# One store per output tile over both 64-row parts, and a last tile that two engines copy out

## The chip, the cores and the metric

The kernel runs on one core of a Trainium2 chip. The metric is the device time of one execution in microseconds (us), the median of several runs. Three runs of the kernel before took 406.9, 407.35 and 407.36 us. One execution was also taken with the hardware profiler; its span is 407.7 us at a mean granted TensorE clock of 0.99, and all times of single instructions come from it.

## The reference

Attention without softmax over 8 batches of 12 heads (448 tokens, head size 64), then a gated feed-forward layer. In short:

```
scores = q @ k.T / 8                       # per batch and head
attn   = maximum(scores, 0)**2 / 448
x      = (attn @ v), heads side by side    # 3584 tokens x 768
gate   = maximum(x @ w_gate, 0)            # 768 x 1536
val    = x @ w_val                         # 768 x 1536
out    = (gate * val) @ w_out              # 1536 x 768, result 3584 x 768 in float32
```

## The kernel before

**Stages.** All engines' programs are written out by the kernel's own planner (`plan`, from L174): it is given operations with their engine, an estimated time, what they depend on, and which buffers they take and read, and it commits one after the other. The instructions are then emitted in order of the planned start. Each engine runs its own list in that order, and waits at an instruction until what it depends on is done. An operation that takes a buffer (`alloc`) waits for the last reader of what was in it.

The batches go in pairs through attention (scores L681, relu L692 or L694, square L704 or L706, product with v L723), the two input products of the feed-forward layer (L787 and L896) and the output product (L1013). From batch 2 on, q and k are transposed by DMA, issued from SyncE (L612). The pairs overlap in time: while the output product of one pair runs, attention of a later one does too.

**Output.** A tile of the result has 128 rows by 384 columns (half of the 768). Its 128 partitions are two groups of 64 tokens. The rows of a batch are laid out so that token `p*7 + t` of the batch is partition p of slot t (`rows`, L973), so a group's 64 rows stand 7 rows apart in the result, and the two groups of a tile are two slots: of the same batch, next to each other, or in some tiles of two batches. There are 56 tiles. The output product of a block of two such tiles is made by a scheme with seven products in place of eight (`out_both`, from L1020), with sums and differences of the hidden tiles (`sh`, L1098, on VectorE), and it ends in one of two ways:

- `evac_add` (L1000): VectorE adds a saved part to what stands in PSUM, and writes a tile `o` in SBUF (L1003).
- `evac` (L992): VectorE or ScalarE, as the planner chooses, copies PSUM to `o` with a scale (`copy_out`, L840; L845 is ScalarE's form, L849 VectorE's).

There are five `o` buffers (the sixth number of `BUFFERS`, L79).

**Stores.** Both ways call `store` (L976), which issues two transfers for a tile, one per group of 64 rows. For most tiles both come from SyncE. For the last four tiles (`last`, L980) the first comes from SyncE and the second from ScalarE. The planner reckons 0.6 us of the issuing engine for each transfer, and 2.5 us until it lands. The last tile of all is written by `evac`, called in `p3_of` (L1125).

Of the kernel before, what the change touches and what calls it, by code (L numbers as in the profile page):

```python
# [57 lines left out]
class Planner:  # L58
# [20 lines left out]
    BUFFERS = (3, 11, 3, 5, 4, 5, 3)  # L79
    PV_PAIRS = (0, 0)  # L80
    JOIN = True
    TWO_QUEUES = True
    SCORES_FIRST = 0.0
    SPLIT = False
    MERGE = False
# [241 lines left out]
def kernel(  # L327
# [10 lines left out]
    nc = tc.nc  # L338
# [3 lines left out]
    B, H, S, D = q.shape  # L342
# [5 lines left out]
    NT = S // P2  # L348
# [7 lines left out]
    OH = d_model // 2  # L356
# [7 lines left out]
    out_scale = lam * lam  # L364
# [7 lines left out]
    ps = psum.tile([128, 8, 512], FP32, name="ps")  # L372
# [19 lines left out]
    o_t = [pool.tile([128, OH], FP32, name=f"o{i}") for i in range(N_O)]  # L392
# [3 lines left out]
    r_x, r_f, r_g, r_o = Res(N_X), Res(N_F), Res(N_G), Res(N_O)  # L396
# [21 lines left out]
    others, pool_ops = [], []  # L418
# [421 lines left out]
    def copy_out(eng, dst, src, scale=None):  # L840
        if eng == "ACT":
            if scale is None:
                nc.scalar.copy(dst, src)  # L843
            else:
                nc.scalar.activation(out=dst, in_=src, func=AF.Copy, scale=float(scale))  # L845
        elif scale is None:
            nc.vector.tensor_copy(dst, src)
        else:
            nc.vector.tensor_scalar_mul(dst, src, float(scale))  # L849
# [123 lines left out]
    def rows(b):  # L973
        return out[b * S:(b + 1) * S, :].rearrange("(p t) m -> t p m", t=NT)

    def store(ob, op, where):  # L976


        slots, hf = where
        last = slots[1] in (((B - 3, 0), (B - 1, 0)) if Planner.JOIN else ((B - 1, NT - 1), (B - 2, NT - 2))) if Planner.TWO_QUEUES else slots[1] == (B - 1, NT - 1)  # L980

        def emit(queue, zs):
            for z in zs:
                bb, t = slots[z]
                queue.dma_start(out=rows(bb)[t][:, hf * OH:(hf + 1) * OH], in_=o_t[ob.idx][64 * z:64 * z + 64])

        for eng, queue, zs in (("SP", nc.sync, (0,)), ("ACT", nc.scalar, (1,))) if last else (("SP", nc.sync, (0, 1)),):
            st = Op({eng: (0.6 * len(zs),) * 2}, lambda queue=queue, zs=zs: emit(queue, zs), deps=[op], reads=[ob])
            st.land = 2.5
            others.append(st)  # L990

    def evac(pb, dep, where, engs=None):  # L992
        ob = Buf(r_o)
        op = Op({"ACT": A384, "DVE": V384}, None, deps=[dep], alloc=[ob], reads=[pb])
        op.emit = lambda: copy_out(op.eng, o_t[ob.idx], ps[:, pb.idx, :OH], out_scale)
        others.append(op)
        store(ob, op, where)
        return op

    def evac_add(pb, dep, fop, fb, where):  # L1000

        ob = Buf(r_o)
        op = Op({"DVE": V384}, lambda: nc.vector.scalar_tensor_tensor(  # L1003
            o_t[ob.idx], ps[:, pb.idx, :OH], float(out_scale), f_t[fb.idx][:, :OH], ALU.mult, ALU.add),
            deps=[dep, fop], alloc=[ob], reads=[pb, fb])
        others.append(op)
        store(ob, op, where)
        return op

    def out_mm(lhs, rhs, pb, start, deps, seg, alloc=(), reads=(), grp=None):  # L1010
        def emit():
            for kf in range(FH):
                nc.tensor.matmul(ps[:, pb.idx, :OH], lhsT=lhs(kf), rhs=rhs(kf), start=start and kf == 0,  # L1013
                                 stop=kf == FH - 1, skip_group_check=True)

        return pe(emit, mm_time(FH, OH), deps=deps, alloc=list(alloc), reads=list(reads), grp=grp)
# [3 lines left out]
    def out_both(b, seg, T_ops):  # L1020
# [11 lines left out]
        nblk = NC + joined  # L1032
# [13 lines left out]
        def tail():  # L1046
            lhs = lambda par: lambda kf: hT[:, 2 * kf + par, S - P2:S + P2]
            A, Bk = bank(), bank()
            slots = ((b, NT - 1), (b + 1, 0))
            even, odd = h_of(pr, (0, 0), (1, 0)), h_of(pr, (0, 1), (1, 1))  # L1050
            a0 = out_mm(lhs(0), w(0, 0), A, True, even + wd, seg, [A], [hb], grp=(pr, "t"))
            fop, fb = snapshot(A, a0, OH, out_scale)
            b0 = out_mm(lhs(0), w(0, 1), Bk, True, even + wd + T_ops, seg, [Bk], [hb], grp=(pr, "t"))

            def rest():
                a1 = out_mm(lhs(1), w(1, 0), A, False, odd + [fop], seg, [], [hb], grp=(pr, "t"))
                b1 = out_mm(lhs(1), w(1, 1), Bk, False, odd + [b0], seg, [], [hb], grp=(pr, "t"))
                evac(A, a1, (slots, 0))
                evac_add(Bk, b1, fop, fb, (slots, 1))
                made.update({(0, "c"): a1, (0, "d"): b1})  # L1060

            made.update({(0, "a"): a0, (0, "b"): b0})
            return rest
# [13 lines left out]
        prev = None  # L1077
        for i in range(nblk + 1):
            cur = None
            if i < nblk:  # L1080
# [11 lines left out]
                for n, a, c, f, parts in (  # L1092
# [4 lines left out]
                    dep = {1: [0], 2: [1]}.get(n, [])  # L1097
                    op = Op({"DVE": (0.46, 0.58)}, lambda n=n, a=a, c=c, f=f: nc.vector.tensor_tensor(sh[n], a(), c(), f),  # L1098
                            deps=of(*parts) + [S_ops[d] for d in dep] + ([prev["S"][n]] if prev and joined else []), alloc=[shb[n]],
                            reads=[hb] + [shb[d] for d in dep])  # L1100
# [6 lines left out]
                           s=tokens,  # L1107
# [14 lines left out]
            def p3_of(prev, i=i):  # L1122
                p3 = made[(i - 1, "3")] = out_mm(prev["sx"](2), w(1, 1), prev["A"], False, [prev["S"][2], o22], seg, [], [prev["shb"][2]],
                            prev["gr"](3))
                evac(prev["A"], p3, (prev["s"][0], 1))  # L1125

            if cur is not None:
                p7 = made[(i, "7")] = out_mm(sx_(3), tw(1), cur["D"], True, T_ops + [S_ops[3]], seg, [cur["D"]], [shb[3]], gr(7))
                cur["p7op"], cur["p7b"] = snapshot(cur["D"], p7, OH, out_scale)
                p2 = made[(i, "2")] = out_mm(hx(1, 0), w(1, 0), cur["E"], True, of((0, 1)) + wd, seg, [cur["E"]], [hb], gr(2))  # L1130
                evac_add(cur["E"], p2, sop, sb, (cur["s"][0], 0))
                if prev is not None:
                    p3_of(prev)
                p6 = made[(i, "6")] = out_mm(sx_(1), tw(0), cur["A"], False, T_ops + [S_ops[1], sop], seg, [], [shb[1]], gr(6))
                cur["uop"], ub = snapshot(cur["A"], p6, OH, out_scale)
                p4 = made[(i, "4")] = out_mm(hx(1, 1), tw(2), cur["D"], False, of((1, 1)) + T_ops + [cur["p7op"]], seg, [], [hb], gr(4))
                evac_add(cur["D"], p4, cur["uop"], ub, (cur["s"][1], 0))
            else:
                p3_of(prev)
            in_order(i)  # L1140
            prev = cur
# [149 lines left out]
```

## Time and profile before

| engine or part | busy us of 407.7 | what it does |
|---|---|---|
| TensorE | 397.1 | all products |
| VectorE | 324.9 | relu, squares, sums, copies |
| ScalarE | 263.0 | relu, squares, copies |
| GpSimd | 75.6 | issues the loads |
| DMA queue 1 (SyncE), all 16 engines | 28.3% | transposes and stores |
| DMA queue 10 (ScalarE), all 16 engines | 0.3% | four stores |
| DMA queue 0 (GpSimd), all 16 engines | 44.0% | loads |

The busy time of an engine is the sum of its instructions' times; a share of DMA is the time that packets took, over the span of 16 DMA engines. These are means over stages with different work. The stores fall in four stretches, about 113 to 150 us, 213 to 251, 309 to 330 and 380 to 405. A VectorE write of an `o` tile takes 557 ns (41 of them), a ScalarE one 490 ns (15). The last store is issued at 404.12 us.

### The profile page before, as it was taken

The page shows a single profiled execution, that of the slowest core. Times are in us where ns is not written, and L with a number is a line of the kernel's source. Part 1 is how long each engine was busy: PE and PEld are TensorE (multiplying, and loading weights), DVE is VectorE, ACT ScalarE, POOL GpSimd, SP SyncE. Part 2 cuts the span into 40 slices and gives each one's busy share as a digit, 9 for nine tenths or more (in the row PEclk, how much of TensorE's full clock was granted, in tenths as well). Part 3 has the DMA queues.
Part 4 walks back from the last instruction along what each step waited for, and adds up shares of the span by engine and source line. Part 5 has one row for each costly group of instructions (what it writes and reads, how often), then busy time and mean ns, then how long its engine had stood idle before and what let it go on. Part 6 is the DMA issues. An engine that isn't in the chain of part 4 may idle for free.

```text
span 407.7 us, 8763 instructions
## 1 busy us (share of the span) xinstructions
PE 397.1 (97%) x3460; PEld 207.2 (51%) x3460; DVE 324.9 (80%) x570; ACT 263.0 (65%) x395; POOL 75.6 (19%) x121
## 2 busy tenths in 40 slices
PE   8789999999999999999999999999999999999995
PEld 4587744444445544444454544444445555555663
DVE  4988674998688798999897998898799657677652
ACT  3878873896686886878587887476686544343221
POOL 7856142122211222102122112110000000000000
PEclk9969999999999999999999999999999999999999
DMA  9999999998779997688878999542002430000244
GB/s 116 187 197 199 200 131 169 159 150 102 92 110 183 142 182 99 74 99 113 82 102 143 168 176 170 76 50 36 2 1 55 100 80 0 2 0 2 72 113 127
DMA packets 77305, 43.44 MB, mean 107 GB/s; under 512 B 40912, under 2 KB 77264, under 8 KB 77264
## 3 DMA queue, kind: packets, MB, share of 16 engines
q0 software_dynamic: 34896, 23.60, 44.0%
q1 hardware_dynamic: 42048, 18.89, 28.3%
q8 instruction: 27, 0.44, 0.4%
q10 hardware_dynamic: 320, 0.39, 0.3%
q14 instruction: 14, 0.11, 0.1%
HBM read 47.19 MB, written 11.01 MB: 143 GB/s over the span
## 4 chain that ended last, share of the span: by engine, by line
PE 91%; DMA 3%; DVE 3%; ACT 2%; issue 0%; ACTq 0%; SPq 0%; DVEq 0%
PE ps L896 36%; PE ps L1013 24%; PE ps L787 12%; PE ps L681 9%; PE ps L723 8%; DMA qkT<-perm 3%; PE ps L1169 2%; ACT at L692 2%; DVE at L694 1%; PE ps L535 1%; PE ps L582 1%; DVE at L706 1%; DVE xT L740 0%; DVE o L1003 0%; DVE hT L938 0%
## 5 line engine op out<-in xcount | busy, mean ns | idle before, releaser
L692 ACT ACTIVATE at<-ps 128x896 bf16<-128x896 f32 (+4 forms) x109 | 94.8, 907 | 17.1 <-PE ps L681 17.0
L843 ACT COPY f<-ps 128x448 f32<-128x448 f32 x100 | 52.8, 531 | 55.3 <-PE ps L896 52.0
L694 DVE TENSOR_SCALAR at<-ps 128x896 bf16<-128x896 f32 (+4 forms) x62 | 66.4, 1073 | 9.5 <-PE ps L681 6.5
L704 ACT ACTIVATE at<-at 128x896 bf16<-128x896 bf16 (+3 forms) x71 | 65.3, 937 | 2.1 <-DVE at L694 1.6
L706 DVE TENSOR_TENSOR at<-at 128x896 bf16<-128x896 bf16 (+3 forms) x100 | 59.0, 613 | 1.1 <-ACT at L692 0.9
L681 PE MATMUL ps<-qkT 64*64 64x448 bf16 (+2 forms) x756 | 51.8, 349 | 3.0 <-DMA qkT<-perm 1.0
L896 PE MATMUL ps<-xT,gvT 128*128 128x448 bf16 x216 | 52.8, 353 | 0.0
L896 PE MATMUL ps<-sx,wv 128*128 128x448 bf16 x216 | 52.2, 353 | 0.0
L896 PE MATMUL ps<-xT,wg 128*128 128x448 bf16 x216 | 51.7, 353 | 0.2 <-DVE at L694 0.2
L896 PEld LDWEIGHTS <-gvT 128*128 128x128 bf16 x324 | 30.0, 98 | 32.6 <-issue 6.9
L1013 PEld LDWEIGHTS <-sh 128*128 128x128 bf16 x312 | 29.2, 98 | 23.7 <-issue 4.2
L422 POOL DMA_DIRECT2D raw<-in_k_dram x18 | 11.3, 628 | 138.9 <-DVE perm L606 113.5
L723 PE MATMUL ps<-at,vv 64*64 64x448 bf16 (+2 forms) x700 | 34.7, 335 | 1.2 <-ACT at L704 0.8
L422 POOL DMA_DIRECT2D vv<-in_v_dram x44 | 26.6, 616 | 49.0 <-PE ps L681 46.4
L1013 PEld LDWEIGHTS <-hT 128*128 128x128 bf16 x270 | 25.5, 98 | 19.9 <-issue 3.6
L1013 PE MATMUL ps<-wo,hT 128*128 128x384 bf16 x192 | 35.5, 327 | 0.0
L681 PEld LDWEIGHTS <-qkT 64*64 64x64 bf16 x756 | 18.9, 109 | 29.3 <-issue 24.5
L845 ACT ACTIVATE f<-ps 128x384 f32<-128x384 f32 x37 | 18.1, 490 | 23.9 <-PE ps L1013 21.0
L787 PE MATMUL ps<-xT,wg 128*128 128x448 bf16 (+2 forms) x180 | 32.7, 319 | 0.3 <-DVE at L694 0.3
L938 DVE TENSOR_TENSOR hT<-ps,g 128x448 bf16<-128x448 f32 x36 | 22.4, 622 | 13.1 <-PE ps L896 12.9
L787 PE MATMUL ps<-xT,wv 128*128 128x448 bf16 (+2 forms) x180 | 32.2, 315 | 0.0
L1003 DVE SCALAR_TENSOR_TENSOR o<-ps,f 128x384 f32<-128x384 f32 x41 | 22.7, 554 | 11.0 <-PE ps L1013 10.2
(70 smaller groups left out, 496.8 us busy)
## 6 DMA issues: line engine op xcount, KB each, us to landing
out_dram<-o SPq DMA_DIRECT2D x108, 96.0 KB, 2.2
vv<-in_v_dram POOLq DMA_DIRECT2D x44, 112.0 KB, 6.9
raw<-in_k_dram POOLq DMA_DIRECT2D x18, 224.0 KB, 4.8
raw<-in_q_dram POOLq DMA_DIRECT2D x18, 224.0 KB, 7.0
wo<-in_moe_w_out_dram POOLq DMA_DIRECT2D x4, 576.0 KB, 12.0
wg<-in_moe_w_gate_dram POOLq DMA_DIRECT2D x5, 384.0 KB, 9.3
wv<-in_moe_w_val_dram POOLq DMA_DIRECT2D x5, 384.0 KB, 10.4
gvT<-in_k_dram POOLq DMA_DIRECT2D x6, 224.0 KB, 6.9
```

What stands on the lines that cost most here:

```text
L422: op = Op({"POOL": (0.5 + 0.0004 * n_desc,) * 2}, lambda: nc.gpsimd.dma_start(out=dst(), in_=src), deps=deps, alloc=alloc)
L681: nc.tensor.matmul(banks()[64 * j:64 * j + 64, z, h2], lhsT=self.k_of(j, h2, k), rhs=self.q_of(j, h2), start=True, stop=True)
L692: nc.scalar.activation(self.at_of(i, m), banks(), AF.Relu)
L694: nc.vector.tensor_scalar_max(self.at_of(i, m), banks(), 0.0)
L704: nc.scalar.activation(a, a, AF.Square)
L706: nc.vector.tensor_tensor(a, a, a, ALU.mult)
L723: nc.tensor.matmul(ps[64 * h2:64 * h2 + 64, ps2.idx + j, :n], lhsT=st.v_of(j, h2, c), rhs=self.at_of(c)[64 * j:64 * j + 64, 0, h2], start= ...
L787: nc.tensor.matmul(ps[:, pb.idx, z * n:(z + 1) * n], lhsT=w[:, kd, fc], rhs=xT_t[xbuf[b].idx][:, kd, cols], start=(kd == 0), stop=(kd == K ...
L843: nc.scalar.copy(dst, src)
L896: nc.tensor.matmul(ps[:, pb.idx, :S], lhsT=w(g)[:, fc], rhs=rhs, start=start and g == 0, stop=stop and g == KH - 1, skip_group_check=True)
L1003: op = Op({"DVE": V384}, lambda: nc.vector.scalar_tensor_tensor(o_t[ob.idx], ps[:, pb.idx, :OH], float(out_scale), f_t[fb.idx][:, :OH], AL ...
L1013: nc.tensor.matmul(ps[:, pb.idx, :OH], lhsT=lhs(kf), rhs=rhs(kf), start=start and kf == 0, stop=kf == FH - 1, skip_group_check=True)
```

## The change

Each tile is stored by one transfer, whose destination is given as an access pattern of two groups by 64 rows by the columns, and whose source is the whole tile of 128 partitions. It takes the place of two issues per tile, and of the special case for the last four tiles. The last tile is copied out by two engines at the same time: VectorE takes the left 192 columns and SyncE stores them, ScalarE takes the right 192 and stores them itself. This is meant to shorten the end of the program, and to halve the issuing work of the queues. The two halves take an `o` buffer each.

```diff
-    TWO_QUEUES = True
...
-    def store(ob, op, where):
+    def store(ob, op, where, eng="SP", cols=(0, OH)):
         slots, hf = where
-        last = slots[1] in (((B - 3, 0), (B - 1, 0)) if Planner.JOIN else ((B - 1, NT - 1), (B - 2, NT - 2))) if Planner.TWO_QUEUES else slots[1] == (B - 1, NT - 1)
-
-        def emit(queue, zs):
-            for z in zs:
-                bb, t = slots[z]
-                queue.dma_start(out=rows(bb)[t][:, hf * OH:(hf + 1) * OH], in_=o_t[ob.idx][64 * z:64 * z + 64])
-
-        for eng, queue, zs in (("SP", nc.sync, (0,)), ("ACT", nc.scalar, (1,))) if last else (("SP", nc.sync, (0, 1)),):
-            st = Op({eng: (0.6 * len(zs),) * 2}, lambda queue=queue, zs=zs: emit(queue, zs), deps=[op], reads=[ob])
-            st.land = 2.5
-            others.append(st)
+        c0, c1 = cols
+
+        def emit():
+            lo, hi = (rows(bb)[t][:, hf * OH + c0:hf * OH + c1] for bb, t in slots)
+            dst = bass.AP(lo.tensor, lo.offset, [[hi.offset - lo.offset, 2]] + [list(x) for x in lo.ap])
+            (nc.scalar if eng == "ACT" else nc.sync).dma_start(out=dst, in_=o_t[ob.idx][:, c0:c1])
+
+        st = Op({eng: (0.6, 0.6)}, emit, deps=[op], reads=[ob])
+        st.land = 2.5
+        others.append(st)
...
-    def evac(pb, dep, where, engs=None):
+    def evac(pb, dep, where, last=False):
+        for eng, queue, c, t in (("DVE", "SP", 0, (0.27, 0.36)), ("ACT", "ACT", OH // 2, (0.24, 0.36))) if last else ():
+            cols = (c, c + OH // 2)
+            ob = Buf(r_o)
+            op = Op({eng: t}, lambda eng=eng, cols=slice(*cols), ob=ob: copy_out(
+                eng, o_t[ob.idx][:, cols], ps[:, pb.idx, cols], out_scale), deps=[dep], alloc=[ob], reads=[pb])
+            others.append(op)
+            store(ob, op, where, queue, cols)
+        if last:
+            return
...
-                evac(prev["A"], p3, (prev["s"][0], 1))
+                evac(prev["A"], p3, (prev["s"][0], 1), b == B - 2 and i == nblk)
```

Apart from this, the instructions of TensorE, VectorE, ScalarE and GpSimd stand in the same order in both programs; SyncE's list is the same with one store where there were two.

## The prediction

> **What bounds the kernel now.** I read the busy shares first, then the table of 40 slices, then the stages in which results are stored, and the end of the chain of waits last.
>
> ```profile
> PE 397.1 (97%) x3460; PEld 207.2 (51%) x3460; DVE 324.9 (80%) x570; ACT 263.0 (65%) x395; POOL 75.6 (19%) x121
> PE   8789999999999999999999999999999999999995
> DMA  9999999998779997688878999542002430000244
> out_dram<-o SPq DMA_DIRECT2D x108, 96.0 KB, 2.2
> ```
>
> TensorE is busy 97% and no slice but the first few and the last leaves it idle: it sets the time. The stores are 108 transfers on SyncE and 4 on ScalarE, landing 2.2 us after issue. The DMA row shows where they fall: beside the loads in slices 12 to 15 and 21 to 25, and alone in slices 31 to 33 and 38 to 40. The next view splits the span at these stages (columns: stretch, length, busy time and count of each engine, clock, DMA share, GB/s).
>
> ```profile
> 113.00:150.00 37.00, 36.88 (x321) 17.91 (x317) 32.30 (x63) 28.12 (x42) 7.30 (x12) 1.00 0.95 151
> 213.00:251.00 38.00, 38.00 (x359) 18.78 (x358) 34.26 (x60) 30.05 (x43) 8.52 (x14) 1.00 1.01 160
> 309.00:330.00 21.00, 21.00 (x155) 11.50 (x154) 15.60 (x33) 9.56 (x16) 0.00 (x0) 1.00 0.41 100
> 380.00:405.00 25.00, 23.27 (x144) 13.79 (x141) 12.20 (x23) 6.37 (x13) 0.00 (x0) 1.00 0.48 119
> ```
>
> The four output stages hold 14, 14, 12 and 16 of the 56 tiles (28, 28, 24 and 32 transfers; each tile is two). In the last two the DMA engines are under half busy, so stores cost TensorE nothing: it is busy 21.00 of 21.00 us. Last, the chain in the final 10 us:
>
> ```profile
> 402.31 0.02 issue
> 402.33 0.57 DVE o L1003
> 402.90 0.02 issue
> 402.93 0.50 ACTq L985
> ...
> 403.60 0.49 ACT o L845
> ```
>
> ScalarE issues a store at 402.93, and only then copies the last tile, from 403.60; its store is issued at 404.12, and the span ends at 407.7. Everything after TensorE's end (402.13 + 1.14 = 403.27) is 4.4 us.
>
> **What the Trainium skill says.** (1) "DMA: Bandwidth & Descriptors", section "Why a DMA increments its semaphore by 16 and not by 1": a DMA is cut along the slowest non-size-1 dimension of its source and of its destination, over the largest number of DMA engines, at most 16, that divides both; for SyncE and ScalarE these are the lowest-numbered ones. The trace agrees for 64-row stores: each left 64 packets of 1,536 bytes and sixteen of 4 bytes, one per engine. It has no outer dimension below 16, so it doesn't show the other half of the rule. (2) The same page, "Rules for kernel authors", advises one 128-partition transfer in place of two over halves of the partitions, because both use the same engines. That speaks for the change, if the one transfer also uses all 16. (3) "Specifications" there: about 27 GiB/s per engine. 65 ns for 1,536 bytes, the commonest packet time on the ScalarE queue in the trace, is 23.6 GB/s, a little less.
>
> **The change, part by part.**
>
> *One store per tile.* The source is 128 partitions. The destination is now [2, 64, 384], with the two row groups outermost, because their distance isn't a multiple of the row step. By (1) the engine count is the largest that divides 128 and 2, which is **two**. The same 196,608 bytes then go as 64 packets on each of two engines, where four packets of each of two transfers went to each of 16. Nothing in the trace shows a two-engine transfer, so I bound a packet: 65 ns with little beside it; and from the stages with stores alone, 0.48 x 16 x 25 us = 192 us for 119 GB/s x 25 us / 1,536 B = 1,937 packets, 99 ns with 16 engines at work. The skill's 27 GiB/s gives 53 ns. I take 65 ns, as fourteen engines are now quiet: **4.16 us per tile** on the same two engines, ends 3.4 and 6.3 us. A tile arrives about every 1.6 us in the last two stages (25 us / 16, 21 us / 12), so stores become the bound there.
>
> *What waits.* There are five o buffers. A copy into one waits until the store of five tiles earlier has landed. That copy stands in VectorE's (or ScalarE's) program order ahead of the sums `sh` of the next block and of the relus and squares, and TensorE waits for those. So the wait passes on to all engines almost whole. On SyncE, DMA transposes stand behind the stores, in the queue and on the two engines.
>
> *Last stage.* First store issued at 380.6; first packet 1.1 us after issue (404.12 to 405.24 for the last store). Five buffers keep the two engines fed. 16 x 4.16 = 66.6, so data ends at 448.3; in the trace the last packet (406.1) precedes the end by 1.6 us: 449.9 against 407.7, **+42**.
>
> *Third stage.* Only the wait for buffers counts, since the rest drains behind the next matmuls. The 12th copy (329.3) needs the 7th landing: 309.4 + 1.1 + 7 x 4.16 + 0.2 = 339.8, **+10.5**.
>
> *First and second stage.* The 14th copy (146.8 and 246.3) needs the 9th landing, 9 x 4.16 = 37.4 us of engine time. But the two engines also carry their sixteenth of the loads and transposes. At the shortest usual time of each packet size in the trace, these fill 0.45 and 0.50 of an engine there, 17 and 19 us. First: 113.5 + 1.1 + 37.4 + 17 = 169, **+22**. Second: 213.3 + 1.1 + 37.4 + 19 = 270.8, **+24.5**. With engines otherwise idle these would be +5 and +6. What is left drains in the 63 us between them.
>
> *Fewer issues.* An issue takes SyncE about 0.55 us; 52 fewer transfers save 29 us on an engine that mostly waits. Nothing, hidden by TensorE. A late effect would be earlier transposes, lost behind the above.
>
> *Last tile in two halves, and ScalarE's issues gone.* ScalarE no longer issues three stores ahead of its last copy, so it can start at about 403.3, not 403.6. The halves cost roughly 0.49 - 192 x 0.64 ns = 0.37 us on ScalarE (slope from 531 ns for 448 columns and 490 for 384) and about the same on VectorE; both then store side by side. Before, the issue came at 404.12; now at about 403.7: **-0.4**, but with two engines the last issue isn't on the path, as the queue ahead of it is 20 us deep. So it is worth nothing in the main case.
>
> Sum: 407.35 + 42 + 10.5 + 22 + 24.5 = 506, say **506 us**.
>
> **The rivals.**
>
> *A: 16 engines after all,* if the program loaded on the chip cuts the two groups differently. Then every store lands in about the 2.2 us of now, TensorE's work is unchanged (the order of all engines' other instructions is the same in both programs), and only -0.4 us of the tail remains: 406.9, at most some tenths lower if transposes issued earlier help. For it: it is what the change wants, and no run here contradicts it. Against it: the rule read literally. This is the rival on the other side, not slower.
>
> *B: two engines, but the first two stages hide it,* because loads run well ahead and leave the two engines alone: only the last two stages and +5 and +6 count, 407.35 + 42 + 10.5 + 11 = 471. With the fast end of a packet (3.4 us per tile) the last stage costs 16 x 0.76 = 12 less, the third +5 and the first two nothing: about 442. Against it: a DMA share of 0.95 and 1.01 in these stages.
>
> *C: two engines, and it compounds.* Transposes wait behind up to five stores, and loads finish only when their shares on these two engines do; the scores of a group of heads begin some 11 us after the first of its two transposes is issued (120.9 to 132.2), a few us after the second lands, which is less than one store. If each of the first two stages costs 25 us more, 556. At 99 ns a packet (6.3 us per tile) the last stage alone is +76, the third +26; with the first two at 60 together, 569.
>
> **How the numbers follow.** I give the main case 0.45, B 0.20, C 0.20 and A 0.15: the rule is stated for this queue and shape, but no run here shows it. The range leaves out A and the far end of C: from 442, the fast end of B, to 575, beyond C's sum. Slower has the three cases with two engines, 0.85. A lies at -0.1% of 407.35, mostly within 0.2% (0.81 us): same 0.09, faster 0.06.
>
> **What would show it.** Right: stores landing in 6 us and more where 2.2 stood, 20 when queued; a DMA share of 2/16 = 0.12 through the last stage with GB/s near 47; copies into o waiting for DMA out_dram<-o by tens of us in total; the chain ending in stores, not in TensorE. The packets would keep 1,536 bytes and their number, but completions would be two 4-byte packets per store. If the stretch from 380 is 25 us long again and stores land in some 2.5 us, the engine count was wrong and A holds. If stores take 6 us and more, but the first two stages keep their length, B; if transposes take 20 us and scores wait for them, C.

## The result, and the profile after

| | median, us | runs |
|---|---|---|
| before | 407.55 | 6 |
| changed | 527.28 | 6 |

The ratio is 1.289, with a 95% interval of 1.2825 to 1.2963: 120 us slower. The profiled run of the changed kernel has a span of 521.7 us.

The same lines of its page as were shown of before (busy times; the slices of TensorE and of the DMA engines), with the granted clock added:

```profile
PE 419.1 (80%) x3460; PEld 210.7 (40%) x3460; DVE 326.8 (63%) x571; ACT 262.7 (50%) x395; POOL 75.8 (15%) x121
PE   8799999999567379999937693999995999995500
PEclk9999999999779879999996896999996999996755
DMA  9999999779866685677949777320011100011111
PE 54%; DMA 29%; DVE 7%; SPq 3%; issue 1%; ACT 1%; DVEq 0%; ACTq 0%
```

The last line is the chain that ended last, as shares of the span. In the page of before it is:

```profile
PE 91%; DMA 3%; DVE 3%; ACT 2%; issue 0%; ACTq 0%; SPq 0%; DVEq 0%
```

VectorE and ScalarE do the same work in the same time as before, but over a longer span. TensorE now has four holes, where results are stored. In the last two stages the DMA row shows 1 tenth, where it showed 2 to 4. In the chain DMA holds 29% of the span, where it held 3%.

The next view gives the stretches between the first and last copies into `o` of each output stage, and those between the stages (columns as in the prediction):

```profile
110.30:164.40 54.10, 40.72 (x311) 18.84 (x308) 31.73 (x61) 25.33 (x38) 7.32 (x12) 0.87 0.74 86
164.40:243.30 78.90, 65.86 (x495) 30.16 (x495) 59.57 (x104) 50.30 (x71) 11.03 (x18) 0.94 0.69 91
243.30:297.30 54.00, 38.53 (x317) 18.25 (x316) 32.43 (x57) 26.67 (x38) 7.34 (x12) 0.89 0.86 89
297.30:372.70 75.40, 66.31 (x463) 30.56 (x463) 52.54 (x92) 43.48 (x66) 3.65 (x6) 0.90 0.42 50
372.70:403.90 31.20, 24.22 (x156) 12.23 (x154) 15.84 (x33) 9.05 (x15) 0.00 (x0) 0.85 0.13 46
403.90:454.30 50.40, 50.40 (x269) 26.35 (x268) 34.67 (x64) 20.49 (x39) 0.00 (x0) 0.99 0.05 20
454.30:521.70 67.40, 28.88 (x144) 14.95 (x142) 12.45 (x24) 6.00 (x13) 0.00 (x0) 0.69 0.13 47
```

The last row is the two engines: a DMA share of 0.13 of 16 is two engines busy all the time, at 47 GB/s for both. TensorE has 28.88 us of work in 67.40. The sixth row has no stores to wait for, and TensorE is busy 50.40 of 50.40.

What the engines waited for (us in total, times, longest):

```profile
ACT o L844 <- DMA out_dram<-o: 66.1, 9, 18.8
DVE o L1010 <- DMA out_dram<-o: 46.4, 14, 8.0
DVE perm L605 <- DMA qkT<-perm: 38.6, 8, 11.8
PE ps L680 <- DMA qkT<-perm: 21.6, 5, 11.8
```

The first two are copies into `o` that wait for an earlier store to land (4.2 us in all in the kernel before). In the other two VectorE's copy ahead of a transpose waits for the transposes before it, and TensorE's scores wait for transposed q and k; in the kernel before these were 0 and 1.0 us. SyncE's queue around the end of the second stage shows why (start, us, queue, operation, count), with the same place of before below it:

```profile
293.99 11.15 SPq L983 DMA_DIRECT2D out_dram<-o  x2
305.25 11.06 SPq L611 DMA_TRANSPOSE qkT<-perm  x2
```

```profile
246.17 3.10 SPq L612 DMA_TRANSPOSE qkT<-perm  x2
```

SyncE spent 11.15 us on issuing two stores and 11.06 on the two transposes behind them. In the kernel before the two transposes took 3.10 us. The end of the chain:

```profile
489.01 0.57 DVE o L1010
...
489.73 14.85 DMA out_dram<-o
504.58 0.02 issue
504.60 0.04 ACTq L844
504.64 0.05 issue
504.69 0.33 ACT o L844
```

A store that is ready at 489.6 lands at 504.58, and only then is there a buffer for the last half tile. Its own store is issued at 505.05, and the span ends 16.7 us later, when the stores still queued on the two engines have landed. The packet records agree with the rule on engines: 7,040 store packets of 1,536 bytes, but two 4-byte packets per store where there were sixteen; in the last stage stores land 3.92 us apart.

### The profile page after: what moved, and what is told of

Its sections match the earlier page's. It is cut to its first block, busy times and chain, and to the rows that moved or that the text cites. A ratio compares the mean times of both kernels' runs of the same rounds, so it can differ in the third digit from the quotient of the medians.

```text
span 521.7 us, 8679 instructions
## 1 busy us (share of the span) xinstructions
PE 419.1 (80%) x3460; PEld 210.7 (40%) x3460; DVE 326.8 (63%) x571; ACT 262.7 (50%) x395; POOL 75.8 (15%) x121
## 3 DMA queue, kind: packets, MB, share of 16 engines
q1 hardware_dynamic: 40688, 19.17, 27.7%
## 4 chain that ended last, share of the span: by engine, by line
PE 54%; DMA 29%; DVE 7%; SPq 3%; issue 1%; ACT 1%; DVEq 0%; ACTq 0%
PE ps L895 27%; DMA out_dram<-o 24%; PE ps L786 9%; PE ps L722 6%; PE ps L1020 6%; PE ps L680 5%; DMA qkT<-perm 5%; DVE at L693 2%; SPq L611 2%; DVE at L705 1%; PE ps L1176 1%; DVE o L1010 1%; SPq L983 1%; ACT at L691 1%; DVE sh L1105 1%
## 5 line engine op out<-in xcount | busy, mean ns | idle before, releaser
L680 PE MATMUL ps<-qkT 64*64 64x448 bf16 (+2 forms) x756 | 52.2, 348 | 32.2 <-DMA qkT<-perm 21.6
L895 PE MATMUL ps<-xT,wg 128*128 128x448 bf16 x216 | 55.5, 373 | 18.9 <-DVE g L947 8.6
L895 PE MATMUL ps<-xT,gvT 128*128 128x448 bf16 x216 | 54.7, 363 | 0.0
L895 PE MATMUL ps<-sx,wv 128*128 128x448 bf16 x216 | 53.4, 359 | 0.0
L1020 PEld LDWEIGHTS <-sh 128*128 128x128 bf16 x312 | 31.1, 104 | 45.6 <-issue 28.6
L1020 PE MATMUL ps<-wo,sh 128*128 128x384 bf16 x156 | 35.1, 369 | 15.1 <-ACT f L844 8.0
L844 ACT ACTIVATE o<-ps 128x384 f32<-128x384 f32 (+1 forms) x15 | 7.2, 482 | 72.2 <-DMA out_dram<-o 66.1
L722 PE MATMUL ps<-at,vv 64*64 64x448 bf16 (+2 forms) x700 | 37.4, 353 | 1.7 <-ACT at L703 0.8
L895 PEld LDWEIGHTS <-wg 128*128 128x128 bf16 x216 | 21.4, 101 | 42.6 <-issue 26.5
L605 DVE COPY perm<-raw 128x1792 bf16<-128x1792 bf16 x18 | 11.2, 622 | 38.6 <-DMA qkT<-perm 38.6
```

The source lines that it names most:

```text
L680: nc.tensor.matmul(banks()[64 * j:64 * j + 64, z, h2], lhsT=self.k_of(j, h2, k), rhs=self.q_of(j, h2), start=True, stop=True)
L722: nc.tensor.matmul(ps[64 * h2:64 * h2 + 64, ps2.idx + j, :n], lhsT=st.v_of(j, h2, c), rhs=self.at_of(c)[64 * j:64 * j + 64, 0, h2], start= ...
L895: nc.tensor.matmul(ps[:, pb.idx, :S], lhsT=w(g)[:, fc], rhs=rhs, start=start and g == 0, stop=stop and g == KH - 1, skip_group_check=True)
```

## The experiments

The theory is the prediction's main case: the destination's outer dimension of 2 puts each store on two DMA engines. The rivals were that one 192 KB transfer is slow by itself, that it matters where the two groups lie in memory, that a part of the loss comes from the split of the last tile, and that a store's time costs in proportion and not only where the engines fall behind. Diffs are against the changed kernel unless they say otherwise. In e2, e3, e5, e6, e10 and e11 rows are placed in other rows of the result, so these kernels don't give the reference's output; each byte is still stored once.

### e1: the store alone

```diff
-                evac(prev["A"], p3, (prev["s"][0], 1), b == B - 2 and i == nblk)
+                evac(prev["A"], p3, (prev["s"][0], 1))
```

> The change without its second part: one store of two groups by 64 rows per tile, but the last tile is copied out by one engine and stored once. Theory (every store runs on two DMA engines, and these two set the end): the second part is worth nothing, as both its halves queue on the same two engines: 527 us, within 3. Rival (the split of the last tile costs a part of the loss, because its second half waits for one more o buffer, 3.9 us later in the trace): 523 us or less. Rival (the split saves its 0.4 us also here): 527.7.

Measured: 525.39 us, ratio 1.2838 (1.278 to 1.2897), within the interval of the whole change. So the store is all of the loss, as far as these runs can tell. The medians differ by 1.9 us, within their noise, so a gain or a loss of one or two us from the split can't be excluded by them. In the two traces the last stage is 67.1 us long without the split and 67.4 with it.

### e2: one store over 128 evenly spaced rows

```diff
-            dst = bass.AP(lo.tensor, lo.offset, [[hi.offset - lo.offset, 2]] + [list(x) for x in lo.ap])
+            even = out[pr * 2 * S:(pr + 1) * 2 * S, :].rearrange("(p t) m -> t p m", t=NT)[t][:, half * OH + c0:half * OH + c1]
```

> One store per tile as in the change, with the last tile in halves, but the destination is 128 rows at one even step, so that its slowest dimension is 128 and not 2. The tiles are placed in other rows of the result for this (each byte once, the same number of bytes and of 1,536-byte rows). Theory (the count of DMA engines is all): the two groups are the whole loss, and 16 engines give rival A of the prediction, 406.9 us, between 406.2 and 407.5; a store lands in 2 to 3 us; 16 packets of 4 bytes per store. Rival (a transfer of 192 KB in one piece lands late by itself, or holds SyncE and the transposes behind it): above 415, with the issue of a store taking over 1 us.

Measured: 407.98 us, ratio 0.9976 (0.9955 to 0.9997). One transfer per tile of the same bytes costs nothing; it even gains 0.2%, as expected, though the interval only just excludes none (the absolute time is above the expected range, as the kernel before took 408.51 us beside it). Its line in the group of `o` (issue times min/median/max in ns) and its row in the table of DMA issues (KB, us to landing):

```profile
L986 SPq DMA_DIRECT2D out_dram<-o x56: 332/332/1019, 110.9 to 400.9; - x56
out_dram<-o SPq DMA_DIRECT2D x55, 192.0 KB, 1.9
```

An issue takes 0.33 us and a tile lands in 1.9, faster than either half did before (2.2). This is rival A of the prediction, which takes a destination whose slowest dimension is 128 and not 2. Three of its stretches, between the first and second stage, between the second and third, and the last stage to the end:

```profile
144.20:210.20 66.00, 65.79 (x509) 30.23 (x508) 61.10 (x107) 50.42 (x72) 12.69 (x21) 1.00 0.83 99
243.70:306.20 62.50, 62.50 (x474) 29.75 (x471) 54.08 (x94) 43.41 (x66) 4.88 (x8) 1.00 0.36 48
377.20:404.10 26.90, 23.30 (x144) 13.80 (x142) 12.58 (x24) 6.23 (x13) 0.00 (x0) 1.00 0.32 118
```

### e3: the same, outer dimension 2

```diff
+            (step, n), col = [list(x) for x in even.ap]
+            even = bass.AP(even.tensor, even.offset, [[step, 2], [step * 2, n // 2], col])
```

> The same as the store over 128 rows at an even step, but with the slowest destination dimension cut to 2: the even rows first, then the odd ones of the 128 (again other rows of the result). Nothing but the outer dimension differs from that kernel, and the addresses of the two parts lie side by side and not 1.3 MB or one row apart. Theory (two engines): 527 us, between 520 and 534, landings 3.92 us apart. Rival (the loss of the change comes from where the two row groups lie in memory): near the even store, 407.

Measured: 527.07 us, ratio 1.2885 to the kernel before. The rows of the two groups now alternate, in the same 128 rows as in e2, and the loss is as in the change. Where the groups lie isn't the cause; the outer dimension is.

### e4: the last tile's split alone

The kernel before, with its stores of 64 rows, and

```diff
+        for eng, c, t in (("DVE", 0, (0.27, 0.36)), ("ACT", OH // 2, (0.24, 0.36))) if last else ():
```

with two stores per half from each engine's queue.

> The kernel before with the second part of the change alone: two stores of 64 rows per tile, the three tiles before the last stored by SyncE and ScalarE as before, and the last tile copied by VectorE and ScalarE, half the columns each, each half stored by its engine's queue in two transfers. Theory (the copy gets shorter by 0.12 us, but each queue now issues two transfers of 0.5 us where it had one, and ScalarE still issues a store until 403.4): 407.4 to 408.0, no gain. Rival (the last copy's length and its engine count, as the prediction took it for 16 engines): 407.0.

Measured: 408.16 us against 408.51, ratio 0.9986 (0.9964 to 1.0008). Nothing that these runs can tell from no change. This doesn't decide between the two expectations, which lie 0.2% apart. The trace speaks for the theory: from the first copy of the last stage to the end it takes 27.7 us, as before.

### e5 and e6: outer dimensions 4 and 8

```diff
+            even = bass.AP(even.tensor, even.offset, [[step, 4], [step * 4, n // 4], col])
```

> As the store over 128 rows at an even step, but with the slowest destination dimension cut to 4 (rows in another order within the 128; each byte once). Theory (four engines, and a store costs only where the engines can't keep up): 32 packets of 61 ns are 1.96 us per tile. In the last stage a tile comes every 1.5 us, so 16 x 1.96 = 31.4 us of data give about +7; in the third stage the seventh landing comes before the 12th copy, 0; in the first two 0 to +2 each: 412 to 420 us, landings 1.96 us apart in the last stage. Rival (a loss in proportion to the time of a store): at 2 engines 3.92 us per tile cost 120 us, at 16 engines 0.49 us cost nothing, so 1.96 us would cost 51: about 459.

> The same with the slowest destination dimension cut to 8. Theory (eight engines, 0.98 us per tile, less than the 1.5 us from tile to tile): no loss but some tenths at the end, 407 to 408.5 us. Rival (in proportion): (0.98 - 0.49) / (3.92 - 0.49) x 120 = +17, 425.

| outer dimension | engines | us, median | ratio to before |
|---|---|---|---|
| 2 (e3) | 2 | 527.07 | 1.2885 |
| 4 (e5) | 4 | 442.28 | 1.0787 (1.0729 to 1.0844) |
| 8 (e6) | 8 | 411.81 | 1.0058 (1.0022 to 1.0094) |
| 128 (e2) | 16 | 407.98 | 0.9976 (0.9955 to 0.9997) |

Neither the theory's 412 to 420 nor the rival's 459 is right for four engines, and eight cost more than the theory's tenths. For the last stage of e5 the theory holds; in its trace stores land 1.96 us apart, and the stage is 36.6 us long against 26.9 in e2, +9.7 (expected +7):

```profile
403.60:440.20 36.60, 23.37 (x144) 13.78 (x141) 12.54 (x24) 6.21 (x13) 0.00 (x0) 0.89 0.24 86
```

A share of 0.24 is four engines of 16, and each store has four 4-byte packets in e5, eight in e6. The third stage lost nothing, as expected. What I missed lies in the first two stages and behind them: +4.9, +5.1, +8.4 and +6.1 us. The wait for an `o` buffer, which is all that the theory counts, explains little of it: in the first stage of e5 no copy into `o` waited for a store, in the second two did, for 2.1 and 7.3 us. These are e5's waits for transposes (us in total, times, longest):

```profile
DVE perm L605 <- DMA qkT<-perm: 17.9, 7, 6.3
PE ps L680 <- DMA qkT<-perm: 14.5, 5, 5.6
```

Of them 16.9 and 12.3 us lie in the first two stages and behind them, and they are the waits that the change has too. In e6 no copy into `o` waits for a store at all. Its second stage is 3.0 us longer than in e2, with waits for transposes of 2.5 us on VectorE and 1.1 on TensorE. Its last stage is 2.0 us longer, and that lies at the end: from the last issue to the end of the span it takes 4.8 us, where e2 takes 2.7.

The packet records show how a few engines fall behind. Where loads and stores are both queued, a packet of a store and one of a load come in turn, of 78 and 87 ns, together every 143 ns: seven store packets a us on each engine, in the change and in e5. At this rate a tile of 128 packets takes 128 / (7 x 4) = 4.6 us on four engines. So the theory was right on the waits for buffers in the last two stages, and left out what else a slow store delays: the transposes, and the end.

### e7: two groups only in the last two stages

```diff
+            if slots[0][0] >= B // 2:
                 dst = bass.AP(lo.tensor, lo.offset, [[hi.offset - lo.offset, 2]] + [list(x) for x in lo.ap])
...
+            else:
+                for z, part in enumerate((lo, hi)):
+                    queue.dma_start(out=part, in_=o_t[ob.idx][64 * z:64 * z + 64, c0:c1])
```

> The stores of two groups by 64 rows only in the last two of the four output stages, two transfers of 64 rows in the first two (last tile in halves as in the change, the output is the same). Theory (each stage pays its own sum): third +10.7 and last +40 as the trace of the change has them, 407.5 + 51 = 458, between 454 and 462; the other 68 us belong to the first two stages and what follows them. Rival (the stages are not independent: a last stage that isn't preceded by delays meets other conditions, a granted clock or loads): off by more than 6 from 458.

Measured: 457.42 us. The two lines of the group of `o` are the two kinds of store in one run, 64 rows on 16 engines and two groups on two:

```profile
L988 SPq DMA_DIRECT2D out_dram<-o x56: 466/586/855, 111.9 to 248.8; - x56
L985 SPq DMA_DIRECT2D out_dram<-o x28: 511/3758/5186, 307.7 to 439.2; - x28
```

The stages add up as the theory has it, to within 1 us.

### e8 and e10: transposes issued from ScalarE

```diff
-                nc.sync.dma_start_transpose(out=qkT_t[st.qt_buf.idx][:, a].rearrange("p j (t c) -> p (j t) c", c=P2),
+                nc.scalar.dma_start_transpose(out=qkT_t[st.qt_buf.idx][:, a].rearrange("p j (t c) -> p (j t) c", c=P2),
```

> The changed kernel with the DMA transposes issued from ScalarE in place of SyncE, at the same places of the plan; stores as in the change. Theory (in the first two stages a good part of the loss is transposes that stand behind stores: in SyncE's program, where the issue of a store takes 3.4 us, and in its queue on the two engines): the time between the first and second output stage and between the second and third, now 13 us longer each than before, comes back to within 5 us of before, and the total is about 527 - 26 = 501, unless ScalarE's new 50 us of issuing cost time themselves. Rival (the two engines' packets delay the transposes whatever queue they stand in): these stretches stay 10 us or more longer, total 515 or more.

> The control for the transposes issued from ScalarE: the same, with the even stores over 128 rows on 16 engines (tiles in other rows of the result). Theory (ScalarE's issuing, some 50 us in front of its relus, costs time by itself): 415 to 430 us, and the loss of two-engine stores beside it is 549 less this, above 119, so that moving the transposes to another queue did not help them. Rival (issuing costs nothing): 408, and the two-engine stores cost 141 with the transposes on ScalarE.

Measured: 549.13 us with the stores of the change (e8), 458.15 with the even stores (e10). With the even stores, moving the transposes to ScalarE costs 50 us by itself (407.98 in e2), more than either expectation of e10 had. So e8's total, which is on its rival's side, says nothing of the transposes alone. Against its control the two-engine stores cost 91 us, not 119. In the two traces the stretches between the stages, 13 us longer each in the change, are 6.1 and 2.5 us longer (83.5 against 77.4, and 72.4 against 69.9); the output stages lose 17.7, 16.2, 10.1 and 40.9. The waits for transposes are almost gone in e8: 0.4 us on TensorE and 0.5 on VectorE, where the change has 21.6 and 38.6. But the issues of the transposes take longer on ScalarE too, first e8, then e10 (ns, min/median/max):

```profile
L611 ACTq DMA_TRANSPOSE qkT<-perm x36: 1245/1696/8027, 51.0 to 359.4; - x36
L611 ACTq DMA_TRANSPOSE qkT<-perm x36: 1246/1468/2602, 52.7 to 319.8; - x36
```

In total they take 88.4 us in e8 and 57.0 in e10. So a part of the loss between the stages goes when the transposes don't stand in SyncE's program, as the theory has it, and slow stores hold up transposes of another queue as well, as the rival has it. How much each is worth in the change isn't separated, as everything in the first two stages also moves more slowly here.

### e11: two transfers, each with outer dimension 2

```diff
+                dst = bass.AP(part.tensor, part.offset, [[step, 2], [step * 2, n // 2], col])
```

for each of the two parts.

> Two transfers of 64 rows per tile as in the kernel before, all from SyncE (the last tile in halves), but each with a slowest destination dimension of 2 (the even rows of the 64, then the odd ones: other rows of the result). Theory (the count of engines, not the count of transfers): the same 64 packets per tile on each of two engines, 527 us, within 6. Rival (one transfer per tile is what costs): near 408.

Measured: 527.43 us. Two transfers per tile or one, on two engines the time is the same. It is the count of engines and not of transfers.

### e9 and e12: versions that keep 16 engines

An output tile whose 128 rows have one step can be stored by one transfer. The same slot of two consecutive batches has it, since a batch is 64 times 7 rows. e9 lays out all hidden tiles that way:

```diff
-        return hT[:, mf, (b % 2) * S:(b % 2 + 1) * S]
+        return hT[:, mf, :].rearrange("p (t z c) -> p t z c", z=2, c=P2)[:, c0 // P2:(c0 + n) // P2, b % 2, :]
...
-                tokens = [tuple((bb, bb % 2 + 2 * it + z) for z in range(2)) for bb in (b, b + 1)]
+                tokens = [tuple((bb, 2 * it + z) for bb in (b, b + 1)) for z in range(2)]
```

> A version that takes what the even store over 128 rows showed and gives the reference's output: the hidden tiles in hT are laid out by slot, with the 64 tokens of both batches of a pair side by side, so that an output tile holds the same slot of two batches; its 128 rows then stand at one even step in the result, and one store over 128 partitions has 128 as its slowest dimension. VectorE writes hT in runs of 64 in place of 448. Theory: 16 engines per store, as in the even store: 0.2% under the kernel before, 407.7 against 408.6 us, if VectorE's writes in runs of 64 take no longer (622 ns for the product from PSUM). Rival (the shorter runs or the plan, which orders some of the attention of the third pair in another way, cost TensorE more than the store gives): 409 us or more.

Measured: 410.01 us, ratio 1.0025 (1.0005 to 1.0045), slower by a quarter of a per cent, on the rival's side. VectorE's writes in runs of 64 take the same 621 ns, which leaves the plan: a tile now needs both batches' hidden tiles. This was not tested apart. In the trace the stretch from the third stage's first copy to the last stage's is 72.3 us against 71.0 in e2, with a wait of TensorE that e2 doesn't have, and the last stage is 27.8 us long against 26.9:

```profile
PE ps L896 <- DVE sx L875: 1.7, 1, 1.7
```

e12 does it only for the tile over both batches, and leaves the plan as it is. The odd batch of each pair after the first is written with its last slot first:

```diff
+                    for c, c0, n in ((P2, 0, S - P2), (0, S - P2, P2)):
+                        nc.vector.tensor_tensor(h_slot(b1, mf)[:, c:c + n], g_t[vb.idx][:, c0:c0 + n], g_t[gb.idx][:, c0:c0 + n], ALU.mult)
...
+            if slots[1][0] > slots[0][0] and slots[1][1] == slots[0][1]:
+                even = bass.AP(lo.tensor, lo.offset, [[lo.ap[0][0], 2 * P2], list(lo.ap[1])])
+                queue.dma_start(out=even, in_=o_t[ob.idx][:, c0:c1])
+            else:
+                for z, part in enumerate((lo, hi)):
+                    queue.dma_start(out=part, in_=o_t[ob.idx][64 * z:64 * z + 64, c0:c1])
```

> Only the tiles whose two groups come from two batches are made even, with the plan's order untouched: from the second pair on, the odd batch's hidden tiles stand in hT with the last slot first, so that the tile over both batches holds slot 6 of each, and its 128 rows have one step. VectorE writes that batch's tiles in two pieces (36 more instructions of 64 columns). These tiles, the last four of the program among them, are stored by one transfer with 128 as the slowest dimension; all others by two transfers of 64 rows, as before; the last tile in halves. The output is the reference's. Theory (16 engines per store, and the gain of the even store lies in the last microseconds alone, where it made the stretch from the first copy of the last stage to the end 26.9 us, from 27.7): 0.1 to 0.2% under the kernel before. Rival (the 36 short instructions on VectorE come before TensorE's products and take the gain back): equal or slower.

Measured: 407.39 us against 408.76, ratio 0.9967 (0.9949 to 0.9985): 0.3% faster than the kernel before, a little more than expected. The six whole tiles, in the group of `o`:

```profile
L988 SPq DMA_DIRECT2D out_dram<-o x6: 332/332/366, 211.2 to 401.4; - x6
```

And the end of the chain:

```profile
401.05 0.37 DVE o L848
401.41 0.03 ACTq L844
401.44 0.04 issue
401.49 0.33 ACT o L844
```

The last store is issued at 401.8, and the span ends at 404.5: from the first copy of the last stage (377.7) to the end 26.8 us, where the kernel before takes 27.7. The two halves aren't copied at the same time: ScalarE's starts when VectorE's has ended (`ACT o L844 <- DVE o L848`, in e2 as well), and the runs don't show why. So both are copied 0.8 us after TensorE's end, no sooner than the whole tile was before (403.27 to 404.09). What is shorter is the time from the last issue to the end of the span, 2.6 us where it was 3.6; a half lands 1.6 us after its issue, where a 64-row store from ScalarE took 2.4. With the split and stores of 64 rows (e4) the stretch was 27.7. So the gain takes the single store; whether it also takes the split was not tried.

## Why the prediction was right, point by point

Every store ran on two engines, as the main case has it, and the time lies in the stated range. That range, 442 to 575 us, takes in almost every case with two engines, so it says little more than that; the main case's 506 us is 21 too low. The table sets its steps beside the stretches of the trace. The measured figures compare the change with e2, which has the same order of work on 16 engines, for the same stretches.

| step of the prediction | predicted, us | measured, us |
|---|---|---|
| first stage | +22 | +20.3 (54.1 - 33.8) |
| between first and second | 0 | +12.9 (78.9 - 66.0) |
| second stage | +24.5 | +20.5 (54.0 - 33.5) |
| between second and third | 0 | +12.9 (75.4 - 62.5) |
| third stage | +10.5 | +10.7 (31.2 - 20.5) |
| between third and last | 0 | -0.1 (50.4 - 50.5) |
| last stage | +42 | +40.5 (67.4 - 26.9) |
| sum | +99 | +117.7 |

- **Two engines**, read from a rule that the trace of before did not show: right, by the two completions per store, by a DMA share of 0.13, and by e2, e3 and e11.
- **The packet.** 65 ns was taken, and most packets are 65 ns long. But in the last two stages stores land 3.92 us apart, 61.3 ns per packet (25.1 GB/s per engine), so packets overlap a little. Over the 16 tiles of the last stage that is 3.8 us too dear. The stage came out only 2.3 us below the forecast of +42 (67.4 - 27.7 against the kernel before itself), partly because the first store lands 6.2 us after its issue, where the sum has 1.1 + 4.16.
- **The five buffers.** In the third stage the wait for the store five tiles earlier gave +10.5, and +10.7 was measured. The mechanism is right; that the figures agree so closely is in part luck. Seven tiles of 3.92 us are 1.7 less than of 4.16, and the first store landed later than reckoned (6.3 us after its issue).
- **The first two stages** came out 2 and 4 us cheaper. The step that added the loads' time to the stores' (0.45 and 0.50 of an engine) was a fair sum of what the engines have to carry. But it isn't all that these stages wait for: TensorE also waited 6.8 us for transposes in the first and 2.6 in the second, which the sum has at nothing.
- **What failed** is the sentence "What is left drains in the 63 us between them". These stretches cost 12.9 us each. The transposes stand there behind the stores that are left: in SyncE's program, which is held at the stores' issue, and on the two engines. The prediction named this and costed it only in case C, at 25 us for each of the first two stages, where it was half of that. With it in the main case the sum would have been 99 + 26 = 125 and the time 532. So the case that came true lies between the main case and C. How the 12.9 us divide between SyncE's program and the engines is open (e8), and a part of the second 12.9 may be a lower clock (see the end).
- **The issues saved** were worth nothing, as said, but the reason given was too kind: on two engines a store's issue takes 3.45 us in the median, where a 64-row one took 0.55. SyncE did not save 29 us of issuing, it lost time.
- **The last tile's halves** were called worth nothing on two engines. e1 agrees within its interval. On 16 engines, -0.4 us was expected; the end of e2 and of e12 is about 0.9 us shorter than before's, with both parts together. The reason given is not what happened: ScalarE's half started 0.48 us after TensorE's end in e12, where the whole tile started after 0.33 before, and the gain lies behind the last issue.

## What to carry to other kernels

Before two transfers are joined in one, read the access pattern from its slowest dimension. Where that counted 2, the transfer ran on two DMA engines here, for 128 rows and for 64 alike (e11), and where it counted 4, on four. A store that is slower than the arrival of tiles wasn't hidden by five buffers: it came back as waits of compute engines for `o`, and as late transposes behind it in the queue. A store that is just faster isn't free either, as e6 took 0.6% more than the kernel before. Arrange the data so that the rows of a tile have one step, as e12 does, and one transfer gives its small gain.

## What the runs showed of the hardware that was not expected

- The issue of a store isn't a fixed cost. It took SyncE 0.33 us for 128 rows at one step, and 0.55 us in the median for 64 rows. For two groups it took 0.51 us for the first three stores of the last stage, and 3.8 us in the median of that stage, about as long as the two engines need for a tile. When they are behind, the issuing queue is held, and all that stands behind it; in e8 transposes on ScalarE's queue were held as well, up to 8.0 us each.
- Packets of a load and of a store come in turn where both are queued: 14 of each a us, for example from 124.5 to 127.5 us in the change, where stores alone run at 32 to 34 on their two engines. Loads become late as well: those of `raw` from k landed after 6.4 us in the median, where it was 4.8.
- The granted TensorE clock of the changed kernel was 0.90 on average, and 0.69 in the last stage, where TensorE was busy for 28.88 of 67.40 us. The same 3,460 matmuls took 419.1 us of busy time, where they took 397.1. In the stretch without stores to wait for, TensorE was never idle, the clock was 0.99 and the length as in e2; in all others of the table it was 0.69 to 0.94. So the lower clock came with the idling. It may have cost a little by itself: between the second and third stage TensorE was busy for 66.31 us, where the same work took 62.50 in e2. No run separates this from the waits.
